# A gated linear attention with a mixture of experts: every engine's order written by hand for the last four attention units and the early expert block

## The chip, the cores and the metric

The kernel runs on one core of a Trainium2 chip. The metric is the device time of one execution in microseconds (us). A core has TensorE (PE) for matmuls, VectorE (DVE), ScalarE (ACT), GpSimd (POOL) and SyncE (SP), each working through its own instructions in their order, and DMA queues that they feed.

## The reference

First an attention-like recurrence for 4 batches, 8 heads, 768 steps and head size 40; then a mixture of 16 experts (4 groups of 4) over its 3072 rows of 320 numbers, where each row goes to the best expert of its best group.

```python
for t in range(S):
    m_new = np.maximum(f_gate[:, :, t] + m, i_gate[:, :, t])
    f_stab, i_stab = np.exp(f_gate[:, :, t] + m - m_new), np.exp(i_gate[:, :, t] - m_new)
    C = f_stab * C + i_stab * einsum('bhd,bhe->bhde', vt, kt)
    n = f_stab * n + i_stab * kt
    y[:, :, t] = sigmoid(o_gate[:, :, t]) * einsum(C, qt) / max(|n . qt|, 1.0)
x = y as 3072 rows of 320
g_idx = argmax(x @ w_group); e_idx = argmax(x[g] @ w_expert[g])   # per row
out[row] = softmax weights of g_idx and e_idx * (max(x[row] @ w1[g, e], 0) @ w2[g, e])
```

## The kernel before

**Attention.** The steps are cut into 6 chunks of 128 and each chunk into its 4 batches, which makes 24 units, numbered 0 to 23 (unit u is chunk u // 4 of batch u % 4). A unit has these steps: `loads` (SP), `decays` (a mask `upper` on POOL, eight exponentials on ACT), `scores` (PE, tile `sp`), `masked` (DVE, tile `pt`, two halves), `carried` and `carried2` (PE `it`, DVE `num`: the part of the state), `values` (PE, `av`), `norm` to `norm3` and `rows` (DVE: the unit's 128 finished rows, tile `x`), `turn` (ACT, SP: the store of `x` to the DRAM tensor `x_d`; PE: three transposes `tp`; ACT: `xT`), and `logits` (PE, `lg`: scores of the 4 groups and 16 experts for each row). A unit's last steps are done during the next unit or the one after.

**Routing.** `route` takes the logits of some units and finds each row's expert, weight and place in the expert's list, on DVE, with an exponential on ACT and some small matmuls on PE (ranks and counts); it is a generator, and the loop takes a piece of it now and then (`go_on`). `put_id` writes 128 rows' numbers and weights (`tokw`) into the lists in DRAM (`itab`), an indirect DMA by POOL. In chunk 4 (units 16 to 19) the route is in two parts, units 16 to 18 and unit 19; in chunk 5 likewise, units 20 to 22 and unit 23.

**The early block.** The two most loaded experts are picked after the third chunk, and their weights loaded and split early (`early_loads`, `early_splits` and `lows`: each fp32 matrix becomes a high part, cast on ACT, and a low part, subtracted on DVE, so that three fast products replace a slow one). The first picked expert does its first 256 rows as soon as the lists of units 0 to 19 are in DRAM: POOL loads its list (`load_ix`, tile `ix`), gathers the rows (`load_x`, tile `xg`, two gathers of 128), PE turns them (`tpm`), ACT and DVE split them (`xhl`), and `early_expert` does both layers (`psh`, then `hh` on ACT and DVE, then `po`). Its 128 late rows are gathered (list `li`) when the last lists are in DRAM, and follow as `expert((0, 1), ...)`. `all_experts` sorts the other 14 experts by load; each is done by `expert` with weights two experts ahead in flight.

**What sets the order.** Up to unit 21 the code's order is each engine's order (`manual_schedule`). Units 22 and 23 and the whole early block stand outside it: there a scheduler orders each engine by its own estimate, guided by `issue_after` and `high_priority`. From `expert((0, 1), ...)` on, the code's order holds again. Two things bear on DRAM order: `no_order` declares stores, gathers and scatters to distinct rows independent, and the second expert's `w2` is the tail of `early_loads`:

```python
    with tc.issue_after(rt["xs"].ins):
        do(early_loads)
```

where `rt["xs"]` is the store of the last unit's `x`. `busy(n)` issues n matmuls whose result nobody reads.

Of the kernel before, what the change touches and what calls it, by code (L numbers as in the profile page):

```python
# [40 lines left out]
CAPS = [EARLY + LATE, 352, 320, 288, 256, 256, 256, 256, 192, 192, 192, 192, 160, 160, 160, 128]  # L41

# [8 lines left out]
def lstm_moe(ctx: ExitStack, tc: tile.TileContext, gates, qkT, nat, og, wcat, w1, w2, cst, out):  # L51
# [55 lines left out]
    rt = {"manual": True}  # L107
# [58 lines left out]
    def decays(u):  # L166
        c, b = divmod(u, B)
        ab = st_[u]["ab"]
        upper(ab, NEG)
# [4 lines left out]
        for j in range(H):  # L174
            rt["exp"] = nc.scalar.activation(ab[:, j, :], ab[:, j, :], AF.Exp, bias=bcol[:, c, b * H + j:b * H + j + 1])  # L175

    def scores(u):
        t = st_[u]
        qk = t["qk"]
        t["pm"] = []  # L180
        for hh in range(2):
# [71 lines left out]
    def values(u):  # L253
        t = st_[u]
        nt = t["nt"]
        av = ps_1.tile([P, 512], F32, name="av")
        for j in range(H):
            o = j * D1
            mm(av[:, o:o + P], t["pm"][j // 4][:, j % 4, :], nt[:, o:o + P], start=True, stop=True)  # L259
        t["av"] = av  # L260
# [22 lines left out]
    def norm3(u):  # L283
# [4 lines left out]
        (nc.gpsimd if u < 20 else nc.vector).tensor_tensor(sr, sigs[c][:, b, :].rearrange("p (h d) -> p h d", d=D),  # L288
# [8 lines left out]
    def turn(u):  # L297
# [3 lines left out]
        rt["xs"] = ins = nc.sync.dma_start(x_d[b * S + c * P:b * S + (c + 1) * P, :], x)  # L301
        if c == NCH - 1:
            no_order("early", ins)
        tp = ps_1.tile([P, 3, P], F32, name="tp", tag="tp")
        for k in range(3):
            kk = min(P, DM - k * P)
            ins = nc.tensor.transpose(out=tp[0:kk, k, :], in_=x[:, k * P:k * P + kk], identity=ident)
        rt["tp", u] = ins
        if u > NU - 4:
            with tc.issue_after(ins.ins):  # L310
                busy(2)
# [8 lines left out]
    def logits(u):  # L320
# [3 lines left out]
        if u == NU - 1:  # L324
            rt["bank"] = ps_1.tile([P, B * 36 + NE], F32, name="lg2", tag="av")
        for k in range(3):
            kk = min(P, DM - k * P)
            rt["lg", u] = mm(rt["bank"][:, b * 20:(b + 1) * 20], st_[u]["xT"][0:kk, k, :], wc[0:kk, k, :],
                             start=(k == 0), stop=(k == 2))
# [7 lines left out]
    def route(c, b0, b1, bank):  # L337
# [11 lines left out]
        with ExitStack() as st:  # L349
            if not rt["manual"] and c == NCH - 2:  # L350
                st.enter_context(tc.issue_after(rt["exp"].ins))
# [507 lines left out]
    def unit(u):  # L859
# [14 lines left out]
        if u < MANUAL:  # L874
            go_on()
# [352 lines left out]
```

## Time and profile before

| | us |
|---|---|
| median of 3 runs | 444.68 (444.68 to 447.98) |
| the profiled execution | 447.25 |
| its span, first to last instruction | 445.7 |
| PE busy | 408.4 |
| DVE busy | 314.1 |
| ACT busy | 270.6 |
| POOL busy | 189.0 |

Times in the rows below are us from the start of the span. The profiled execution is 2.57 us longer than the median and 1.55 us longer than its own span. The attention part ends near 180 us, the early block runs to about 215 us, the other 14 experts take the rest. On the page's 40 slices the PE row stands at 9 nearly throughout; the slice that begins at 178 us stands at 4.

### The profile page before, as it was taken

The page shows a single profiled execution, that of the slowest core. Times are in us where ns is not written, and L with a number is a line of the kernel's source. Part 1 is how long each engine was busy: PE and PEld are TensorE (multiplying, and loading weights), DVE is VectorE, ACT ScalarE, POOL GpSimd, SP SyncE. Part 2 cuts the span into 40 slices and gives each one's busy share as a digit, 9 for nine tenths or more (in the row PEclk, how much of TensorE's full clock was granted, in tenths as well). Part 3 has the DMA queues.
Part 4 walks back from the last instruction along what each step waited for, and adds up shares of the span by engine and source line. Part 5 has one row for each costly group of instructions (what it writes and reads, how often), then busy time and mean ns, then how long its engine had stood idle before and what let it go on. Part 6 is the DMA issues. An engine that isn't in the chain of part 4 may idle for free.

```text
span 445.7 us, 9295 instructions
## 1 busy us (share of the span) xinstructions
PE 408.4 (92%) x3324; PEld 390.2 (88%) x3324; DVE 314.1 (70%) x731; ACT 270.6 (61%) x602; POOL 189.0 (42%) x215
## 2 busy tenths in 40 slices
PE   7599999997998999499999999999999999999970
PEld 4599999986997998299999999999999999999960
DVE  6755876658759798375474656756677999999950
ACT  5559556485476653134473655755676888888840
POOL 7454657474664472425523224234223333343120
PEclk9989999998999899689999999999999999999995
DMA  5998987989599941535385566386567676777000
GB/s 155 305 302 279 305 193 217 300 216 278 163 316 306 318 153 37 171 136 165 124 317 193 183 239 203 133 306 215 193 237 273 236 244 233 257 283 280 17 24 1
DMA packets 29908, 94.73 MB, mean 213 GB/s; under 512 B 9169, under 2 KB 13226, under 8 KB 26276
## 3 DMA queue, kind: packets, MB, share of 16 engines
q1 hardware_dynamic: 24804, 79.59, 55.5%
q0 software_dynamic: 4784, 14.18, 9.2%
q8 instruction: 27, 0.44, 0.4%
q10 hardware_dynamic: 272, 0.36, 0.3%
q14 instruction: 21, 0.17, 0.1%
HBM read 84.14 MB, written 10.82 MB: 213 GB/s over the span
## 4 chain that ended last, share of the span: by engine, by line
PE 63%; issue 11%; POOL 9%; DVE 7%; DMA 4%; ACT 1%; POOLq 0%; SPq 0%; DVEq 0%; ACTq 0%
PE psh L690 24%; PE po L733 6%; PE po L734 6%; PE po L735 6%; PE sp L185 4%; PE po L739 2%; PE psh L710 2%; PE po L738 2%; PE psh L631 2%; POOL sr L288 2%; PE it L211 2%; DMA xg<-x_d,ix 2%; POOL kw L198 2%; POOL itab L453 2%; DMA w1s<-in_w_dram 1%
## 5 line engine op out<-in xcount | busy, mean ns | idle before, releaser
L551 POOL DMA_INDIRECT out_dram<-y,ix x34 | 44.8, 1319 | 132.6 <-ACT y L747 121.3
L690 PE MATMUL psh<-xhl,w1h 128*128 128x256 f32 (+4 forms) x368 | 85.4, 309 | 0.0
L175 ACT ACTIVATE ab<-ab,bcol 128x128 f32<-128x128 f32 x184 | 56.3, 388 | 13.9 <-POOL ab L147 13.3
L733 PE MATMUL po<-w2h,hh 128*128 128x320 f32 (+1 forms) x192 | 60.7, 316 | 0.0
L690 PEld LDWEIGHTS psh<-xhl,w1h 128*128 128x128 f32 x368 | 59.9, 189 | 0.0
L734 PE MATMUL po<-w2l,hh 128*128 128x320 f32 (+1 forms) x192 | 59.3, 309 | 0.0
L735 PE MATMUL po<-w2h,hh 128*128 128x320 f32 (+1 forms) x192 | 59.2, 308 | 0.0
L664 DVE TENSOR_TENSOR w2l<-w2s,w2h 128x640 fp32r<-128x640 f32 x64 | 51.8, 823 | 6.4 <-ACT w2h L660 5.4
L185 PE MATMUL sp<-qk 128*128 128x128 f32 x384 | 50.9, 287 | 4.9 <-DMA qk<-in_qkT_dram 4.9
L259 PE MATMUL av<-nt,pt 128*128 128x128 f32 x384 | 51.7, 288 | 0.9 <-DVE pt L191 0.8
L185 PEld LDWEIGHTS sp<-qk 128*128 128x128 f32 x384 | 47.3, 200 | 5.7 <-issue 2.8
L690 PE MATMUL psh<-xhl,w1l 128*128 128x256 f32 (+6 forms) x256 | 49.0, 273 | 0.0
L259 PEld LDWEIGHTS av<-nt,pt 128*128 128x128 f32 x384 | 46.6, 197 | 2.4 <-DVE pt L191 1.4
L783 DVE SCALAR_TENSOR_TENSOR hh<-psh,hh 128x512 fp32r<-128x512 f32 (+3 forms) x36 | 21.5, 615 | 36.5 <-ACT hh L780 36.5
L690 PE MATMUL psh<-xhl,wsk 128*128 128x256 f32 (+4 forms) x184 | 46.8, 304 | 0.0
L147 POOL TENSOR_SCALAR_AFFINE_SELECT ab<-ab 128x1024 f32<-128x1024 f32 (+1 forms) x25 | 27.1, 1083 | 45.0 <-DMA ab<-a_d 38.3
L660 ACT CAST w2h<-w2s 128x640 fp32r<-128x640 f32 x64 | 45.0, 723 | 0.0
L547 POOL DMA_INDIRECT xg<-x_d,ix x34 | 36.1, 1061 | 18.6 <-DMA ix<-itab 7.1
L690 PEld LDWEIGHTS psh<-xhl,w1l 128*128 128x128 f32 x256 | 42.5, 189 | 0.0
L664 DVE TENSOR_TENSOR w1l<-w1s,w1h 128x1024 fp32r<-128x1024 f32 x32 | 38.9, 1219 | 3.7 <-ACT w1h L660 3.6
L191 DVE TENSOR_TENSOR pt<-sp,ab 128x512 f32<-128x512 f32 x48 | 32.9, 685 | 10.2 <-PE sp L185 8.2
L780 ACT ACTIVATE hh<-psh 128x512 fp32r<-128x512 f32 (+3 forms) x28 | 18.0, 644 | 31.0 <-PE psh L690 31.0
(183 smaller groups left out, 888.0 us busy)
## 6 DMA issues: line engine op xcount, KB each, us to landing
w1s<-in_w_dram SPq DMA_DIRECT2D x12, 1536.0 KB
w2s<-in_w_dram SPq DMA_DIRECT2D x13, 1280.0 KB
ab<-a_d SPq DMA_DIRECT2D x23, 512.0 KB
nt<-in_nat_dram SPq DMA_DIRECT2D x24, 324.0 KB
qk<-in_qkT_dram SPq DMA_DIRECT2D x48, 160.0 KB
x_d<-x SPq DMA_DIRECT2D x24, 192.0 KB
sig<-in_og_dram SPq DMA_DIRECT2D x6, 640.0 KB
w1s<-in_w_dram SPq DMA_DIRECT2D x4, 768.0 KB
```

The lines of the kernel that those rows point to most:

```text
L175: rt["exp"] = nc.scalar.activation(ab[:, j, :], ab[:, j, :], AF.Exp, bias=bcol[:, c, b * H + j:b * H + j + 1])
L185: mm(sp[:, jj, :], qk[:, j % 2, j // 2, :], qk[:, 2, j // 2, :], start=True, stop=True)
L191: nc.vector.tensor_tensor(pt, t["pm"][hh], t["ab"][:, 4 * hh:4 * hh + 4, :], op=ALU.mult)
L259: mm(av[:, o:o + P], t["pm"][j // 4][:, j % 4, :], nt[:, o:o + P], start=True, stop=True)
L547: return nc.gpsimd.indirect_dma_start(out=o, out_offset=None, in_=src, in_offset=bass.IndirectOffsetOnAxis(ap=idx, axis=0))
L551: return nc.gpsimd.indirect_dma_start(out=out, out_offset=bass.IndirectOffsetOnAxis(ap=idx, axis=0), in_=y, in_offset=None, bounds_check=N ...
L660: nc.scalar.copy(t[names[0]][:, dst], src[r][:, s])
L664: nc.vector.tensor_tensor(o, src[r][rows, s], h.bitcast(F32), op=ALU.subtract)
L690: mm(ps[:, g, 0:n_], w[:, s], x, start=(n == 0), stop=(n == len(todo) - 1))
L733: mm(po[0:m], hh[:, f, t], w2h[:, s], start=st0, stop=False)
L734: mm(po[0:m], hh[:, f, t], w2l[:, s], start=False, stop=False)
L735: mm(po[0:m], hh[:, f, tl], w2h[:, s], start=False, stop=sp0)
```

## The change

The scheduler's part is gone: units 20 to 23 are written out in `last_units`, and the early block's side work in the generator `lists`, of which `early_expert` takes a piece after every half and every whole pair of feature blocks. The last units are routed as 16 to 18, 19, 20 and 21, 22 and 23. Unit 19's `logits` stand in unit 20 and its route in units 20 and 21. The low parts of the first expert's w2 (three of four), until now in units 20 to 23, stand in the early block between the `hh` steps, and the selection of the experts behind them. The third expert's `w1` and `w2` are asked for after the gathers for the second. `turn` of the late rows stands before the last two of the eight feature blocks, formerly before the third. The store of `x` and the gathers are declared independent of each other but not among themselves.

```diff
-        (nc.gpsimd if u < 20 else nc.vector).tensor_tensor(sr, sigs[c][:, b, :].rearrange("p (h d) -> p h d", d=D),
+        (nc.gpsimd if u < HAND - 1 else nc.vector).tensor_tensor(sr, sigs[c][:, b, :].rearrange("p (h d) -> p h d", d=D),
...
-        ends = {B - 1: 0} if c < NCH - 2 else {B - 2: 0, B - 1: B - 1}
-        if b in ends:
-            chores.insert(0 if c < NCH - 2 else len(chores), route(c, ends[b], b + 1, rt["bank"]))
+        if b == B - 1 and c < NCH - 2:
+            chores.insert(0, route(c, 0, B, rt["bank"]))
...
                 for n, (w, s, x) in enumerate(todo):
                     mm(ps[:, g * W:(g + 1) * W], w[:, s], x, start=(n == 0), stop=(n == len(todo) - 1))
+                if g == 0:
+                    steps(lists, 1)
...
+            steps(lists, 1)
+        after()
...
-                if f == NF // 4 and i == len(blocks(W)) - 1:
-                    with tc.issue_after(ins.ins):
-                        do(last)
+                if f == NF - 2 and i == len(blocks(W)) - 1:
+                    do(last())
...
-        for _ in range(1 if u < 20 else 3):
+        for _ in range(4 if u == HAND - 1 else 1):
             put_id()
+
+    def last_units():
+        a, b, c, d = range(HAND, NU)
+        loads(d)
+        decays(c, "upper")
+        norm(a - 1)
+        scores(a)
+        norm1(a - 1)
+        masked(a, 0)
+        norm2(a - 1)
+        carried(a)
+        logits(a - 2)
+        r1 = route(NCH - 2, 0, B - 1, rt["bank"])
+        masked(a, 1)
+        norm3(a - 1)
+        rows(a - 1)
+        steps(r1, 1)
+        carried2(a)
+        steps(r1, 3)
+        values(a, (0,))
+        turn(a - 1)
+        values(a, (1,))
+        steps(r1, 1)
+        logits(a - 1)
+        r2 = route(NCH - 2, B - 1, B, rt["bank"])
+        decays(c, "exp")
+        steps(r1, 5)
+        put_ids()
+        steps(r1, 1)
+
+        norm(a)
+        scores(b)
+        steps(r2, 4)
+        norm1(a)
+        masked(b, 0)
+        steps(r2, 1)
+        carried(b)
+        steps(r2, 3)
+        masked(b, 1)
+        steps(r2, 2)
+        put_ids()
+        decays(d, "upper")
+        load_ix(0, nc.gpsimd)
+        xgs[0] = load_x(EARLY, ix_of(0), True)
...
+        carried(d)
+        logits(b)
+        r3 = route(NCH - 1, 0, 2, rt["bank"])
+        masked(d, 1)
+        steps(r3, 4)
+        carried2(d)
+        norm3(c)
+        rows(c)
+        values(d, (0,))
+        steps(r3, 1)
+        values(d, (1,))
+        turn(c)
+        xl = early_turn((0, 0), EARLY, xgs[0], ((ps_a, "it"), (ps_s, "sp")))
+        norm(d)
+        norm1(d)
+        norm2(d)
+        norm3(d)
+        rows(d)
+        do(xl)
+        logits(c)
+        steps(r3, 5)
+        put_ids()
+        busy(2)
+        turn(d)
+        do(early_loads)
+        steps(r3, 1)
+        busy(2)
+        logits(d)
+        rt["r4"] = route(NCH - 1, 2, B, rt["bank"])
+        steps(rt["r4"], 4)
...
+        def lists():
+            steps(rt["r4"], 6)
+            put_ids()
+            lreg = nc.values_load(late_i[0:1, 0:1], engines=[ET.SP], min_val=0, max_val=NSLOT - P,
...
+            xgs[0, 1] = load_x(LATE, rt["late"])
+            xgs[1] = load_x(CAPS[1], ix_of(1))
+            yield
+            for _ in range(2):
+                yield
+                do(lows, 1)
+                yield
+            yield
+            do(lows)
+            experts = all_experts()
+            next(experts)
+            load_e(2, [ET.SP, ET.Pool])
+            load_ix(2)
+            load_w1(2, nc.gpsimd)
+            load_w2(2, nc.gpsimd)
+            yield
+            next(experts, None)
+            yield
```

How this moves instructions, at three places.

POOL, at the entries of unit 19 into the lists (`itab`), before:

```order
L453 DMA itab<-tokw,slot 49280x2
L452 MEMSET sep 1x1 x5
L453 DMA itab<-tokw,slot 49280x2
L580 ISA
L580 DMA ix<-itab 128x3x2
L547 DMA xg<-x_d,ix 128x384 x2
L453 DMA itab<-tokw,slot 49280x2 x4
L557 TENSOR_LOAD ewi
L565 ISA
L565 DMA w1s<-in_w_dram 128x3072
```

and after:

```order
L447 DMA itab<-tokw,slot 49280x2
L446 MEMSET sep 1x1
L447 DMA itab<-tokw,slot 49280x2
L150 AFFINE_SELECT ab<-ab 128x1024
L579 ISA
L579 DMA ix<-itab 128x3x2
L546 DMA xg<-x_d,ix 128x384 x2
L446 MEMSET sep 1x1
L447 DMA itab<-tokw,slot 49280x2
```

Unit 19's entry, the list's load and the gathers keep their sequence; the mask of unit 23 (AFFINE_SELECT) now stands between the entry and the list's load, which before stood ahead of all of these.

PE, where the gathered rows are turned (`tpm`), before:

```order
L374 LDWEIGHTS ones_b
L374 MATMUL lg<-ohsum_77,ones_b 128x48
L328 MATMUL lg_2554<-wc,xT 128x20
L611 MATMUL tpm<-cs,xg 128x128 x6
L114 LDWEIGHTS ones_b
L114 MATMUL busy<-ones_b 128x512
```

and after:

```order
L267 MATMUL av<-nt,pt 128x128 x4
L314 MATMUL tp<-cs,x 128x128 x2
L314 MATMUL tp<-cs,x 64x128
L610 MATMUL tpm<-cs,xg 128x128 x6
L329 MATMUL lg<-wc,xT 128x20 x3
L117 LDWEIGHTS ones_b
L117 MATMUL busy<-ones_b 128x512
```

The transposes of the gathered rows stood behind every unit's `logits` (`lg_2554` is unit 23's) and directly ahead of the first expert product; now they stand behind unit 22's `tp`, with the logits of units 22 and 23 and unit 23's `tp` behind them.

DVE, from a step `hh` of the early expert to the late rows' low part `xhl`, before:

```order
L634 SCALAR_TENSOR_TENSOR hh<-psh,hh 128x2x256
L535 TENSOR_TENSOR ovr<-cntr,off 128x16
L536 TENSOR_SCALAR ovr<-ovr 128x16
L538 CAST ovi<-ovr 128x16
L539 TENSOR_SCALAR ovi<-ovi 128x16
L540 CAST ovr<-ovi 128x16
L542 TENSOR_REDUCE tot_f<-ovr 128x1
L543 CAST total<-tot_f 128x1
L634 SCALAR_TENSOR_TENSOR hh<-psh,hh 128x2x256 x2
L664 TENSOR_TENSOR w1l<-w1s,w1h 128x1024 x2
L664 TENSOR_TENSOR wsk<-w1s,wsk 64x1024
L614 TENSOR_TENSOR xhl<-tpm,xhl 128x3x128
```

and after:

```order
L528 TENSOR_TENSOR big<-sel,cntf 128x256
L529 TENSOR_REDUCE cntr<-big 128x16
L534 TENSOR_TENSOR ovr<-cntr,off 128x16
L535 TENSOR_SCALAR ovr<-ovr 128x16
L537 CAST ovi<-ovr 128x16
L538 TENSOR_SCALAR ovi<-ovi 128x16
L539 CAST ovr<-ovi 128x16
L541 TENSOR_REDUCE tot_f<-ovr 128x1
L542 CAST total<-tot_f 128x1
L667 TENSOR_TENSOR w1l<-w1s,w1h 128x1024 x2
L667 TENSOR_TENSOR wsk<-w1s,wsk 64x1024
L613 TENSOR_TENSOR xhl<-tpm,xhl 128x3x128
```

Before, two `hh` steps stood between the last selection step (`total`) and the low parts of the second expert's w1; now the fourth `hh` stands ahead of the whole second half of the selection, and that directly ahead of `w1l`.

## Rows read from the trace of the kernel before

**Rows 1.** Windows of the span. Columns: stretch (us from the span's start); its length and PE's busy time with the count of instructions; then PEld, DVE, ACT and POOL in the same way; the granted clock of TensorE (1.00 is its upper level of 2.4 GHz, 0.50 its lower of 1.2 GHz); the DMA share; GB/s.

```profile
180.00:185.00 5.00, 1.19 (x5) 0.69 (x5) 1.59 (x10) 0.48 (x1) 3.16 (x4) 0.66 0.90 321
...
185.00:190.00 5.00, 3.07 (x11) 1.77 (x12) 1.42 (x10) 0.60 (x2) 0.00 (x0) 0.50 0.03 8
...
215.00:236.00 21.00, 21.00 (x142) 20.75 (x141) 12.86 (x16) 11.94 (x19) 9.50 (x10) 1.00 0.69 234
```

**Rows 2.** The timeline of PE from the last units to the first expert product. Columns here and in every timeline below: start, length (us), engine, line, operation, output<-input, shapes, count, and in brackets how long the engine stood idle before and what ended it.

```profile
176.21 0.95 PE L328 MATMUL lg<-wc,xT 128*128 128x20 f32 x6
...
177.96 0.52 PE L307 MATMUL tp<-cs,x 128*128 128x128 f32 x3 [0.80 <-DVE df L347]
...
179.90 0.40 PE L328 MATMUL lg<-wc,xT 64*128 64x20 f32 x2
...
182.86 0.90 PE L611 MATMUL tpm<-cs,xg 128*128 128x128 f32 x3 [2.57 <-DMA xg<-x_d,ix]
...
186.76 0.90 PE L611 MATMUL tpm<-cs,xg 128*128 128x128 f32 x3 [3.00 <-DMA xg<-x_d,ix]
...
189.11 0.98 PE L631 MATMUL psh<-xhl,w1h 128*128 128x256 f32 x3 [0.17 <-DVE oh L361]
```

**Rows 3.** The timeline of POOL: the last list entry of unit 19, the list's load, the first gather, the last list entry of all, the late gather.

```profile
170.61 1.29 POOL L453 DMA_INDIRECT itab<-tokw,slot  x1 [2.37 <-DVE tokw L405]
...
174.85 0.81 POOL L580 DMA_DIRECT2D ix<-itab  x1 [2.95 <-DMA itab<-tokw,slot]
...
177.97 1.00 POOL L547 DMA_INDIRECT xg<-x_d,ix  x1 [2.32 <-DMA ix<-itab]
...
191.48 0.96 POOL L453 DMA_INDIRECT itab<-tokw,slot  x1 [6.69 <-DVE slot L403]
...
197.12 1.00 POOL L547 DMA_INDIRECT xg<-x_d,li  x1 [1.40 <-DMA li<-itab]
```

**Rows 4.** The gather's line L547 in the stretch from 170 to 215 us, its last line: from issue to landing.

```profile
DMA to landing us min/median/max: 3.6/4.6/7.4
```

**Rows 5.** The timeline of SP's queue: five stores of x, then the two halves of the second expert's w2.

```profile
158.42 20.02 SPq L301 DMA_DIRECT2D x_d<-x  x5
...
178.64 0.88 SPq L565 DMA_DIRECT2D w2s<-in_w_dram  x2
```

**Rows 6.** The timeline of ACT: the eight exponentials of unit 23's decays, then the route of unit 19; and the first relu of the early expert.

```profile
165.76 2.44 ACT L175 ACTIVATE ab<-ab,bcol 128x128 f32<-128x128 f32 x8
...
168.11 0.20 ACT L352 ACTIVATE ex<-df 128x20 f32<-128x20 f32 x1
...
192.68 0.60 ACT L633 ACTIVATE hh<-psh 128x512 fp32r<-128x512 f32 x1 [4.38 <-PE psh L631]
```

**Rows 7.** The timeline of DVE: the last step of the route of units 16 to 18, and that of unit 19.

```profile
163.22 0.15 DVE L405 TENSOR_TENSOR tokw<-sm,se 128x3 f32<-128x3 f32 x1
...
170.18 0.15 DVE L405 TENSOR_TENSOR tokw<-sm,se 128x1 f32<-128x1 f32 x1
```

**Rows 8.** One window: from unit 20's scores to the end of unit 22's logits (columns as in rows 1).

```profile
151.00:177.16 26.16, 25.63 (x218) 24.13 (x216) 22.54 (x86) 14.15 (x38) 12.30 (x22) 1.00 0.45 143
```

**Rows 9.** The timeline of DVE: first and last step of the four that turn logits into one-hot rows, of units 20 to 22.

```profile
177.20 0.22 DVE L345 TENSOR_REDUCE mx<-lg 128x15 f32<-128x60 f32 x1
...
178.76 0.21 DVE L365 TENSOR_TENSOR oh<-oh 128x48 bf16<-128x48 f32 x1
```

**Rows 10.** One window: the first expert's first layer, 64 matmuls and a few small ones (columns as in rows 1).

```profile
189.11:198.11 9.00, 9.00 (x70) 8.91 (x70) 7.22 (x36) 1.80 (x3) 2.52 (x3) 0.85 0.19 54
```

**Rows 11.** The timeline of PE: the first matmul of the early expert's second layer, the transposes of the late rows, the first matmul of the late block.

```profile
198.11 0.31 PE L645 MATMUL po<-w2h,hh 128*128 128x320 f32 x1
...
202.57 0.55 PE L611 MATMUL tpm<-cs,xg 128*128 128x128 f32 x3
...
205.60 0.28 PE L690 MATMUL psh<-xhl,w1h 128*128 128x256 f32 x1
```

**Rows 12.** The timeline of DVE: one quarter of a w2 low part; then, in the early block, the first and the last step of the expert selection with one hh and the six equal small steps' first among them, the low parts of the second expert's w1, and the late rows' low part.

```profile
163.38 0.82 DVE L664 TENSOR_TENSOR w2l<-w2s,w2h 128x640 fp32r<-128x640 f32 x1
...
190.51 0.17 DVE L459 SCALAR_TENSOR_TENSOR key<-cntf,keyb 128x16 f32<-128x16 f32 x1
...
193.31 0.69 DVE L634 SCALAR_TENSOR_TENSOR hh<-psh,hh 128x512 fp32r<-128x512 f32 x1 [0.65 <-ACT hh L633]
...
195.84 0.17 DVE L535 TENSOR_TENSOR ovr<-cntr,off 128x16 f32<-128x16 f32 x1
...
197.08 0.15 DVE L543 CAST total<-tot_f 128x1 int32<-128x1 f32 x1
...
199.87 2.36 DVE L664 TENSOR_TENSOR w1l<-w1s,w1h 128x1024 fp32r<-128x1024 f32 x2 [0.24 <-ACT w1h L660]
...
202.26 1.22 DVE L664 TENSOR_TENSOR wsk<-w1s,wsk 64x1024 fp32r<-64x1024 f32 x1
...
203.68 0.56 DVE L614 TENSOR_TENSOR xhl<-tpm,xhl 128x384 fp32r<-128x384 f32 x1 [0.19 <-ACT xhl L613]
```

**Rows 13.** The timeline of PE: the end of the longest other wait of the attention part.

```profile
105.97 0.19 PE L370 MATMUL lg<-oh,lt_b 128*128 128x64 bf16 x1 [3.01 <-DVE oh L365]
```

**Rows 14.** Two windows of 1 us after it (columns as in rows 1).

```profile
106.00:107.00 1.00, 1.00 (x15) 1.00 (x15) 0.85 (x5) 1.00 (x5) 0.00 (x0) 0.74 1.04 421
...
109.00:110.00 1.00, 1.00 (x7) 1.00 (x7) 0.72 (x4) 0.00 (x0) 0.00 (x0) 0.55 0.98 266
```

More of the change, by code (lines that the diff above doesn't have):

```diff
@@ L613, in one, with early_expert @@
             nc.scalar.copy(xh, tp[:, :, 0:m])
-            nc.vector.tensor_tensor(xhl[:, :, 1, i * P:i * P + m], tp[:, :, 0:m], xh.bitcast(F32), op=ALU.subtract)
-        return [lambda i=i, m=m: one(i, m) for i, m in enumerate(blocks(W))]
-    def early_expert(W, ws, idx, after, last):
+            t["low"].append(lambda: nc.vector.tensor_tensor(xhl[:, :, 1, i * P:i * P + m], tp[:, :, 0:m],
+                                                            xh.bitcast(F32), op=ALU.subtract))
+        for i, m in enumerate(blocks(W)):
+            one(i, m)
+        return t["low"]
+    def early_expert(W, ws, idx, lists, after, last):
         w1h, w1l, wsk, w2h, w2l = (ws[n] for n in ("w1h", "w1l", "wsk", "w2h", "w2l"))
@@ L918, in unit, with steps @@
             gate_o(u // B + 1)
-        for _ in range(1 if u < 20 else 3):
+        for _ in range(4 if u == HAND - 1 else 1):
             put_id()
+    def steps(g, n):
+        for _ in range(n):
+            next(g, None)
+    def last_units():
[40 more added lines that the diff above has]
+        xgs[0] = load_x(EARLY, ix_of(0), True)
+        norm2(a)
+        carried2(b)
+        norm3(a)
+        rows(a)
+        steps(r2, 1)
+        values(b)
+        do(early_splits, 2)
+        norm(b)
+        scores(c, (0,))
+        turn(a)
+        scores(c, (1,))
+        decays(d, "exp")
+        norm1(b)
+        masked(c, 0)
+        norm2(b)
+        carried(c)
+        logits(a)
+        masked(c, 1)
+        carried2(c)
+        norm3(b)
+        rows(b)
+        values(c, (0,))
+        turn(b)
+        values(c, (1,))
+        do(early_splits)
+        steps(early_counts(), 9)
+        norm(c)
+        scores(d)
+        norm1(c)
+        masked(d, 0)
+        norm2(c)
+        carried(d)
[28 more added lines that the diff above has]
+        steps(rt["r4"], 4)
@@ L1022, in lstm_moe @@
     with tc.manual_schedule():
-        for u in range(2, MANUAL):
+        for u in range(2, HAND):
             unit(u)
@@ L1070, in lstm_moe @@
-    load_ix(1)
-    load_e(2, [ET.SP, ET.Pool])
-    load_ix(2)
-    next(experts, None)
-    for r in range(NEARLY):
-        xgs[r, 1] = load_x(LATE, late_ix[r])
-    xgs[1] = load_x(CAPS[1], ix_of(1))
-    load_w1(2, nc.gpsimd)
-    load_w2(2, nc.gpsimd)
-    own, rest = casts(1)
-    def second_w1():
-        for act, low in own:
-            act()
-            low()
-    early_expert(EARLY, wsp_[0], ix_of(0), second_w1, turn_tasks((0, 1), LATE, xgs[0, 1]))
-    pools["ps_o_"].close()
-    first_banks.close()
@@ new lines, in second_w1 @@
+        def second_w1():
+            for act, low in own:
+                act()
+                low()
+        early_expert(EARLY, wsp_[0], ix_of(0), lists(), second_w1, lambda: early_turn((0, 1), LATE, xgs[0, 1], [(ps_1, "tp")]))
+        early_banks.close()
+        first_banks.close()
+        pools["ps_h"] = enter(tc.tile_pool(name="ps_h2", bufs=3, space=PSUM, reuse_waits="tile"))
+        pools["ps_o"] = enter(tc.tile_pool(name="ps_o2", bufs=2, space=PSUM, reuse_waits="tile"))
+        pools["late"] = True
@@ L1094, in lstm_moe @@
+        expert((0, 1), LATE, rt["late"], [], (), lambda: turn2(1, CAPS[1], xgs[1]))
         own = rest
```

164 lines of the change are left out of this document (61 added, 103 removed).

## The prediction

> **What bounds the kernel now.** I read the page's slices first: PE is busy almost throughout, with one hole at 178 to 189 us. The windows show the hole and what surrounds it: PE works 1.19 of the 5 us from 180 and 3.07 of the next 5, at a granted clock of 0.66 and 0.50, while in the experts' stage it is busy 21.00 of 21 us at full clock [rows 1]. So a microsecond won before about 205 us reaches the end whole, if it is won on PE. The hole's causes are on PE's timeline: the last unit's logits end at 180.3, the gathered rows arrive in two pieces at 182.86 and 186.76 (idle 2.57 and 3.00, both ended by the gather's DMA), and the first expert product starts at 189.11 [rows 2]. The chain behind it lies on POOL: unit 19's entry into the lists at 170.61, released by DVE's `tokw`; the list's load 4.24 later; the first gather 3.12 after that [rows 3]. A gather of this stretch lands 3.6 us after its issue at best, 4.6 in the median, 7.4 at worst [rows 4]. The worst one is the second gather of the hole; the second expert's w2 goes out at 178.64, in the middle of it [rows 5].
>
> **The change part by part.**
>
> *Unit 19 routed at once.* Before, its exponential stood on ACT behind the eight of unit 23's decays and began at 168.11 [rows 6], so `tokw` came at 170.18, while the route of units 16 to 18 was ready at 163.22 [rows 7]. Now its logits precede unit 21's scores and its DVE steps follow those of units 16 to 18, with one unit's `pt`, `num` and `x` between. I put its `tokw` at about 163.5, an estimate: the time at which the first part ended before, since the first part no longer shares DVE with two w2 low parts. Entry 163.8; the mask of unit 23, now between entry and list load, ends while the entry lands; list load 168.0, gathers 171.2 and 172.5, the second landed between 176 and 177 (180 with the worst latency). The w2 transfer still goes out behind the last store of x, as it did before [rows 5]: this third of the change moves no instruction past another on SP, and is worth only the separation that the earlier gather gives.
>
> *PE up to the first product.* From unit 20's scores to unit 22's logits PE was busy 25.63 of 26.16 us [rows 8], so the new order can't gain there; it can lose. It works through the same matmuls; two turned blocks come in and four idle fillers go out, which I call even. New waits that the written order makes, walked through engine by engine: unit 19's small rank matmuls wait for their one-hot rows behind unit 21's scores (about 0.9); the half-unit interleaving of `turn` and `values` waits for x (0.2 to 0.3, three times); the ranks of units 20 and 21 stand between the halves of unit 23's `values` and wait for one-hot rows that can't begin before unit 21's logits (0.5). From logits to one-hot rows is 1.77 us on DVE [rows 9], some 1.3 of it without the other unit's work between. The sum is 2.0 to 2.4 more than the 0.5 idle before: unit 22's logits end at 179.2 instead of 177.1. Before, the last unit's logits ended 3.1 later [rows 2]; with 2.3 here, since the fillers and the transposes of unit 23 lie in what was waiting, the first product starts at **181.5, not 189.11: 7.6 earlier**. The gather's 177 is just in time for its place ahead of unit 22's logits (178).
>
> *First layer.* It took 9.00 us at a mean clock of 0.85 [rows 10], so 7.65 at full clock. New in it: the ranks of units 22 and 23 stand after the first eight matmuls (under 1 us) and wait for their one-hot rows, which start only when the last logits are out and DVE has finished the route of 20 and 21: 1.0 of waiting. 8.65, to 190.1 instead of 198.11.
>
> *Second layer and the late block.* From there to the late block's first product was 7.49 us, all of it PE work [rows 11]; PE would be ready at 197.6. But the late rows' low part `xhl` must be there, and DVE's queue now reaches it later. Before, the three w2 low parts (0.74 us from one start to the next [rows 12]) lay in the attention part, and the selection between the `hh` steps while PE multiplied. Now DVE does hh, w2l, hh, w2l, hh, w2l, the selection's first half, the fourth hh, its second half, w1l twice, wsk, xhl. The third hh starts at 189.0 (third product pair at 188.25, ACT's relu 0.6 [rows 6]): 0.6 for it, 0.75 for w2l. The selection from `key` to `total` took 6.7 from 190.51 to 197.23 with two `hh` of 0.6 in it, 0.65 idle and two small strangers, so 4.65 alone; one hh on top makes 5.25 [rows 12]. That is 195.6. Then w1l and wsk, 3.6 from 199.87 to the end of wsk, and xhl 0.56 [rows 12]: 199.7. The steps that depend on each other lose the fillers that stood between them, 0.3 to 0.6: **200.2**. PE idles 2.5 us at the late block, which starts 5.4 earlier than 205.60. The late gather itself is not the bound: the last entry of a list goes out near 187, and 5.64 later [rows 3] the gather, landed by 197.
>
> *The clock.* A hole of this size has a price of its own. The longest other one, 3.01 us before 105.97 [rows 13], was followed by a granted clock of 0.50 from about 106.5 to 109.5 [rows 14], that is 1.2 instead of 2.4 GHz for 3.0 us of work-bound time: 1.5 us lost. The holes of 2.57 and 3.00 in question did the same [rows 1, 2]. Holes of 0.5 in all, in the last attention units, cost nothing: the clock there is 1.00 [rows 8]. 2.5 is nearer to the former, so I charge the 1.5.
>
> Sum: 5.4 - 1.5 = 3.9. The profiled execution becomes 447.25 - 3.9 = 443.35; it lay 2.57 above the median, and the forecast against the median is 444.68 - 3.9 = **440.8**. Everything after the late block is taken as unmoved: each weight load is released by a cast that PE's progress paces, and the third expert's w1, now asked for behind the gathers, has some 15 us until its first cast.
>
> A figure that would change this: the Trainium skill, Perfetto Trace Analysis, section "Optimizing Scalar/DVE Operations", states about 60 ns of access overhead for a DVE instruction on SBUF and a profiled latency of about twice that. The six equal steps from 195.84 to 197.08 stand 0.21 apart [rows 12], hence the trace doesn't agree for steps that depend on each other. By the page's 0.12, an estimate, some twenty such steps would be 1.8 shorter, the hole 0.7, the clock would hold, and the sum would be 7.2: 437.5.
>
> **The rivals.**
>
> *The clock holds through the hole.* A fall needs more than a gap: The 0.80 us before 177.96 [rows 2] passed without one until the next hole came. If 2.5 after 16 us of dense work passes too, the gain is 5.4: 439.3.
>
> *DVE is not late.* Were the selection to run in 3.0 us instead of 5.25, by steps that overlap, xhl would be ready when PE is and the gain would be nearly the whole 8.0 by which PE is ready earlier (205.60 less 197.6), 437. For it speaks only that DVE idled 0.65 among these steps before, so that some of their spacing is not their own. The Trainium skill's figure above, in Perfetto Trace Analysis, is this case.
>
> *The hand order waits more than walked.* Each unit has five handovers between PE, ACT and DVE, and the old scheduler overlapped two units freely; at 0.1 more for each of twenty handovers the first product comes 2 us later, and PE, thinned out around 180, falls to the lower clock once more for 1.5. Gain 3.9 - 3.5 = 0.4: 444.3.
>
> *Slower: the gather is no earlier.* `tpm` now stands ahead of the logits of units 22 and 23 and of unit 23's transposes, which before were done by 180.3. If the gathered rows land as late as before, at 186.7, these are behind them: about 4.5 at the lower clock to the first product, 191.2, so 2.1 late instead of 7.6 early, with the 1.0 and 2.5 of the two new waits on top: 450.3. The mechanism would be a list load that waits on POOL for a transfer that is not among those on POOL's timeline [rows 3]. It decides from a landing at about 183 on; my walk has 177.
>
> *It doesn't do what it says* holds for w2 alone, as said, and costs nothing.
>
> **How the numbers follow.** Forecast with the clock falling 0.42 (440.8; by the bounds of the waits 439.8 to 442.2); clock holding 0.27 (439.3); DVE not late 0.08 (437); more waits 0.17 (444.3); slower 0.06 (450). A measurement of this kernel tells about 1% from no change, 4.4 us: faster than 440.2 are the second and third case and a seventh of the first, 0.41; over 449.1 lies only the last, 0.05 of it; the rest 0.54. The range leaves out the slower case and the outer halves of the two next: 437.5 to 444.3.
>
> **What would show it.** Right: unit 19's list entry near 164 on POOL and both gathers landed before 178; PE's first expert product at 181 to 182 without a wait of over 1 us on a gather; a wait of PE for DVE's `xhl` of 2 to 3 us at the first late product, near 200; granted clock at 0.50 for some 3 us after it. Wrong: gathers still the last thing before the first product; a late block that starts straight behind the second layer (then the gain is larger); or several holes between 157 and 181 (then smaller).

## The result, and the profile after

The changed kernel takes 449.11 us in the median of 19 runs (445.01 to 454.39), the kernel before 444.72 beside it. The ratio is 1.008, with a 95% interval of 1.0052 to 1.0109: slower by 0.5 to 1.1%, where 440.8, 0.9% faster, was forecast. Runs that the chip disturbed are left out of the ratios, and where the profiled run of a kernel below is such a one (the second bank, the pause with three moves), only stretches of it are read. The profiled execution took 451.05 us, its span is 449.5 (445.7 before).

PE's timeline around the new first product, with its waits in brackets; it answers to [rows 2]:

```profile
151.82 1.95 PE L191 MATMUL sp<-qk 128*128 128x128 f32 x16
...
157.76 0.87 PE L314 MATMUL tp<-cs,x 128*128 128x128 f32 x3 [1.33 <-DVE mx L345]
...
164.31 0.17 PE L367 MATMUL lg<-oh,lt_b 128*128 128x16 bf16 x1 [0.69 <-DVE oh L362]
...
170.35 0.55 PE L314 MATMUL tp<-cs,x 128*128 128x128 f32 x3 [1.80 <-DVE x L301]
...
182.67 0.82 PE L610 MATMUL tpm<-cs,xg 128*128 128x128 f32 x6
...
186.47 0.92 PE L329 MATMUL lg<-wc,xT 128*128 128x20 f32 x6 [0.88 <-DVE pr L395]
187.32 0.74 PE L633 MATMUL psh<-xhl,w1h 128*128 128x256 f32 x4
```

The gathered rows are no bound any more: `tpm` starts without a wait. Yet the first product comes at 187.32, 1.8 us earlier than before (189.11), not 7.6. From unit 20's scores at 151.82 it is 35.50 us (38.1 before). The two longest waits stand ahead of the turns of units 19 and 20. (The first is put down to `mx`, the step that starts behind `x` on DVE; `x` of unit 19 ended at 157.61, 0.15 ahead of the turn.) DVE and POOL show why. First DVE, then POOL, around the finished rows of unit 20 (and `sr` of unit 19 and of unit 21 for comparison; `sr` is the output gate divided by `den`, the last thing that `x` needs):

```profile
155.26 1.82 DVE L295 TENSOR_TENSOR sr<-sig,den 128x320 f32<-128x320 f32 x1
...
167.69 2.08 DVE L295 TENSOR_TENSOR sr<-sig,den 128x320 f32<-128x320 f32 x1
169.80 0.49 DVE L301 TENSOR_TENSOR x<-num,sr 128x320 f32<-128x320 f32 x1
...
173.32 0.49 DVE L295 TENSOR_TENSOR sr<-sig,den 128x320 f32<-128x320 f32 x1
```

```profile
155.63 1.10 POOL L150 TENSOR_SCALAR_AFFINE_SELECT ab<-ab 128x1024 f32<-128x1024 f32 x1
...
167.34 0.95 POOL L447 DMA_INDIRECT itab<-tokw,slot  x1 [1.09 <-DVE den L288]
168.30 1.11 POOL L150 TENSOR_SCALAR_AFFINE_SELECT ab<-ab 128x1024 f32<-128x1024 f32 x1
...
172.31 0.81 POOL L579 DMA_DIRECT2D ix<-itab  x1 [2.89 <-DMA itab<-tokw,slot]
...
176.17 1.00 POOL L546 DMA_INDIRECT xg<-x_d,ix  x1 [3.05 <-DMA ix<-itab]
177.47 0.95 POOL L546 DMA_INDIRECT xg<-x_d,ix  x1 [0.30 <-issue]
```

The same product of the same size takes 0.49 us for unit 21, but 1.82 and 2.08 for units 19 and 20, and both long ones end 0.35 us after a mask on POOL ends. PE's turn needs `x`. Unit 19's `sr` is on DVE by the change itself: before, POOL did it, in 0.72 at 155.82.

At the early block's end, the last work of DVE and the late block's first product (they answer to [rows 12] and [rows 11]), then the clock (columns as in [rows 1]):

```profile
202.33 0.15 DVE L542 CAST total<-tot_f 128x1 int32<-128x1 f32 x1
202.44 2.36 DVE L667 TENSOR_TENSOR w1l<-w1s,w1h 128x1024 fp32r<-128x1024 f32 x2
204.83 1.22 DVE L667 TENSOR_TENSOR wsk<-w1s,wsk 64x1024 fp32r<-64x1024 f32 x1
206.08 0.56 DVE L613 TENSOR_TENSOR xhl<-tpm,xhl 128x384 fp32r<-128x384 f32 x1
```

```profile
206.70 0.58 PE L693 MATMUL psh<-xhl,w1h 128*128 128x256 f32 x1 [2.63 <-DVE xhl L613]
...
213.99 1.07 PE L713 MATMUL psh<-cs,xg 128*128 128x128 f32 x9
```

```profile
155.00:160.00 5.00, 3.67 (x22) 3.45 (x22) 4.69 (x15) 3.13 (x9) 1.74 (x3) 0.77 0.94 280
160.00:165.00 5.00, 4.31 (x39) 4.01 (x39) 3.33 (x18) 3.06 (x9) 2.11 (x4) 0.89 0.26 67
...
205.00:210.00 5.00, 3.30 (x15) 3.31 (x16) 1.97 (x3) 0.37 (x1) 2.71 (x4) 0.55 0.92 320
210.00:215.00 5.00, 5.00 (x37) 5.00 (x36) 1.98 (x7) 2.06 (x6) 0.00 (x0) 0.77 0.90 350
```

The late block starts 1.1 us later than before (206.70 for 205.60) and its first layer takes 7.29 instead of 4.65 us at the fallen clock. 1.1 + 2.64 is 3.74 of the 3.8 by which the span grew. So all that the change gained ahead of the hole was given back in DVE's queue, and in this execution the hole then cost the clock as well.

### The profile page after: what moved, and what is told of

It reads as the page before. It is cut to its first block, busy times and chain, and to the rows that moved or that the text cites. A ratio compares the mean times of both kernels' runs of the same rounds, so it can differ in the third digit from the quotient of the medians.

```text
span 449.5 us, 9283 instructions
## 1 busy us (share of the span) xinstructions
PE 409.5 (91%) x3319; PEld 392.0 (87%) x3319; DVE 321.9 (72%) x730; ACT 270.7 (60%) x602; POOL 187.3 (42%) x214
## 4 chain that ended last, share of the span: by engine, by line
PE 65%; DVE 12%; DMA 8%; issue 5%; POOL 5%; SPq 1%; ACT 1%; POOLq 0%; DVEq 0%; ACTq 0%
PE psh L693 24%; PE po L736 6%; PE po L737 6%; PE po L738 6%; PE sp L191 5%; PE av L267 3%; DMA nt<-in_nat_dram 2%; PE po L742 2%; PE psh L713 2%; PE it L217 2%; PE lg L329 2%; PE po L741 2%; DMA qk<-in_qkT_dram 2%; DMA itab<-tokw,slot 2%; DMA a_d<-A__117 2%
## 5 line engine op out<-in xcount | busy, mean ns | idle before, releaser
L693 PE MATMUL psh<-xhl,w1h 128*128 128x256 f32 (+4 forms) x368 | 87.5, 314 | 2.6 <-DVE xhl L613 2.6
L693 PEld LDWEIGHTS psh<-xhl,w1h 128*128 128x128 f32 x368 | 61.4, 193 | 2.9 <-DVE xhl L613 2.9
L267 PE MATMUL av<-nt,pt 128*128 128x128 f32 x384 | 52.6, 289 | 0.8 <-DVE pt L197 0.7
L693 PE MATMUL psh<-xhl,w1l 128*128 128x256 f32 (+6 forms) x256 | 49.9, 277 | 0.0
L693 PEld LDWEIGHTS psh<-xhl,w1l 128*128 128x128 f32 x256 | 43.8, 194 | 0.0
```

What stands on the lines that cost most here:

```text
L267: mm(t["av"][:, o:o + P], t["pm"][hh][:, jj, :], nt[:, o:o + P], start=True, stop=True)
L693: mm(ps[:, g, 0:n_], w[:, s], x, start=(n == 0), stop=(n == len(todo) - 1))
```

## The experiments

The theory: two things put the time where it is. A mask on GpSimd holds up a VectorE product beside it, which makes units 19 and 20 late, and VectorE's queue makes the late block late and drops the clock. Rivals: the waits are the price of the written order as such, or they are hidden by the gather or by the next wait. Times are read in two ways. The first is the median and its ratio to the kernel before, measured beside it; that kernel's own median was 444.72 beside the changed kernel and 445.13, 446.02 and 446.92 beside the experiments, so two kernels of different groups are compared by their ratios. The changed kernel's is 1.008, and a difference of less than about 0.5% between two ratios is not told from nothing. The second, since single runs of one kernel lie 5 us apart, is the distance from unit 20's scores to the first product in the profile (35.50 in the changed kernel).

**Masks earlier.** Both masks before the entries of units 16 to 18.

```diff
         loads(d)
-        decays(c, "upper")
...
-        decays(c, "exp")
+        decays(d, "upper")
+        decays(c, "upper")
         steps(r1, 5)
         put_ids()
...
         steps(r2, 4)
+        decays(c, "exp")
...
         put_ids()
-        decays(d, "upper")
         load_ix(0, nc.gpsimd)
```

> Edit: POOL's masks of units 22 and 23 are issued ahead of the list entries of units 16 to 18, in a stretch where POOL waits, instead of next to the DVE steps sr of units 19 and 20; unit 22's exponentials move behind unit 19's. Theory (POOL's mask and list entry hold DVE up: sr took 1.82 and 2.08 us beside them, 0.49 elsewhere): sr of unit 19 about 0.5 to 0.9, sr of unit 20 at most 1.1 (only the list entry is still beside it); PE's waits of 1.33 and 1.80 us for x of these units fall under 0.8 each, the clock does not fall near 158, the first expert product comes 2 to 3.5 us earlier, at 184 to 185.5, and the time falls by as much. Rival (sr is slow for what it reads or because of its place in DVE's queue): both sr stay at 1.8 to 2.1, the time stays.

455.02 us, ratio to the kernel before 1.0224 (1.0123 to 1.0325). `sr` fell to 0.49 and 0.75 and the waits for `x` to 0.33 and 1.07, so the hold-up is the masks' (the 0.75 stands beside one of them still). But POOL now waited for unit 23's decays, with the list entries queued behind:

```profile
163.60 2.13 POOL L150 TENSOR_SCALAR_AFFINE_SELECT ab<-ab 128x1024 f32<-128x1024 f32 x2 [8.35 <-DMA ab<-a_d]
...
177.33 0.80 POOL L579 DMA_DIRECT2D ix<-itab  x1 [6.38 <-DMA x_d<-x]
```

```profile
183.15 0.52 PE L610 MATMUL tpm<-cs,xg 128*128 128x128 f32 x3 [3.05 <-DMA xg<-x_d,ix]
```

The list load starts 5 us later than in the changed kernel, and the rows arrive after PE wants them. The last list entry went out 2.4 later (169.75 for 167.34); the row puts the end of the wait down to a store of `x`, and which of the two landings it was is not settled. This is the prediction's slower rival (the gather no earlier, with the logits queued behind `tpm`), brought about by the experiment: its price was real, its place was elsewhere.

**A bank of their own for the last logits.**

```diff
+        if u == NU - 2:
+            rt["bank"] = ps_1.tile([P, B * 36 + NE], F32, name="lg2", tag="av")
```

> Edit: the logits of units 22 and 23 go to a PSUM bank of their own, as unit 23's did in the kernel before. Theory (the last logits wait for DVE's product pr of the route of units 20 and 21 because both use one bank): the wait of 0.88 us at 186.47 goes, and the first expert product comes 0.7 to 0.9 earlier; time down by 0.5 to 1. Rival (they wait for ACT's copy xT of unit 23): the wait stays, the time stays.

448.73 us, 1.0084 (1.0037 to 1.013). The wait of 0.88 is gone; the wait of the ranks behind it grew from 0.37 to 0.68. From the turn of unit 20 to those ranks it is 18.09 instead of 18.55 us, so some 0.5 is won, which the ratio does not tell from nothing. Its profile shows two more things. Both `sr` are held as in the changed kernel (1.83 and 2.08), yet the clock stays at 1.00 from 155 to 220. The distance is 33.21, of which the wait of 0.88 explains 0.88: with that wait it would be 34.1. So some 1.4 of the changed kernel's 35.50 is the clock's fall behind unit 19, which did not come here although both masks are where they were. And behind the hole at the late block, 2.56 here, the clock did not fall either, and the first layer took 4.74:

```profile
210.05 0.39 PE L695 MATMUL psh<-xhl,w1h 128*128 128x256 f32 x1 [2.56 <-DVE xhl L615]
```

```profile
210.00:215.00 5.00, 4.95 (x42) 4.95 (x43) 1.93 (x5) 1.76 (x6) 1.37 (x2) 1.00 0.97 399
```

**Second half of the selection behind `xhl`.**

```diff
                     do(last())
+                    next(rt["experts"], None)
...
             yield
-            next(experts, None)
+            rt["experts"] = experts
             yield
```

> Edit: the second half of the expert selection stands behind the late rows' low part xhl on DVE, not ahead of the second expert's w1 low parts. Theory (the hole of 2.63 us ahead of the late block is DVE's queue, and the clock's fall after it costs as much again): xhl comes 3 to 3.9 earlier, the hole shrinks to what the late gather leaves (0.5 to 1), the clock stays at 1.00 through 205 to 215, the late block takes 4.7 us instead of 7.3, and the time falls by 4 to 5. Rival (the hole ends with the late gather or with ACT): hole 2 us or more, time within 1 us of the changed kernel's.

445.06 us, 1.0036 (1.0001 to 1.0071), by fourteen small steps on DVE moved behind four others: 4.05 below the changed kernel by the medians, 2.0 by the ratios, whose intervals just overlap. The hole is 0.28 instead of 2.63 (the late gather is waited for 0.74 instead of 0.51), and the clock holds:

```profile
202.85 0.39 PE L694 MATMUL psh<-xhl,w1h 128*128 128x256 f32 x1 [0.28 <-DVE xhl L613]
```

```profile
205.00:210.00 5.00, 4.71 (x40) 4.50 (x39) 4.10 (x16) 2.85 (x9) 1.14 (x2) 1.00 0.98 392
210.00:215.00 5.00, 5.00 (x35) 5.00 (x34) 1.47 (x4) 1.20 (x3) 1.10 (x2) 1.00 0.61 210
```

The late block's first layer takes 5.30 instead of 7.29, and not the 4.7 expected, since PE now waits for DVE within it (0.6 in all).

**Twelve idle matmuls in the hole.** They stand behind the last product of the second layer, and nobody reads them.

```diff
+        fl = ps_1.tile([P, 512], F32, name="fill", tag="lg")
+        for _ in range(12):
+            mm(fl, ones_b, bc(ones_b.unsqueeze(1), (P, 4, P)), start=True, stop=True)
```

> Edit: twelve fillers of 0.215 us (matmuls whose result nobody reads) stand in PE's order between the second layer and the late block, in the hole; nothing else moves. Theory (the hole itself costs 2.6, the clock's fall behind it another 2.6): the late block starts when xhl is there, as before, but runs in 4.7 us instead of 7.3 and the clock stays at 1.00; time down by 2 to 2.7. Rival (the clock falls anyway for the thin work before, or the late block is slow because of its own waits): the late block still takes over 6 us, time as the changed kernel's or 0.3 worse.

446.17 us, 1.0047 (1.0008 to 1.0086): 2.9 below the changed kernel by the medians, 1.5 by the ratios, with `xhl` as late as there. The clock of the two windows above is 1.00 and the late block's first layer takes 4.69. In the changed kernel's profile the clock's share of the hole's price, 2.64, is as much as the wait. That the idle matmuls keep the clock up is supported by the time as well, but one profile doesn't prove it, since with the second bank it stayed up without them.

**Mask of unit 23 behind the list load,** and its exponentials behind the turn of unit 21.

```diff
         put_ids()
-        decays(d, "upper")
         load_ix(0, nc.gpsimd)
+        decays(d, "upper")
...
-        decays(d, "exp")
...
         turn(b)
+        decays(d, "exp")
```

> The changed kernel with one thing moved: GpSimd masks unit 23's decays between the list load and the gathers (in the changed kernel it does so right behind the last list entry, at 168.30), and ScalarE's eight exponentials of that unit come behind the turn of unit 21 instead of before it. Theory A (a GpSimd mask beside a VectorE product of two SBUF operands holds the product up until the mask is over): unit 20's sr takes 0.5 to 1.0 us instead of 2.08, PE's wait for x of unit 20 falls from 1.80 to 0.3 to 0.8, the gathers start no later than 176.2 and 177.5, and the time falls by 1.0 to 1.5 us against the changed kernel (to about 447.7). Theory B (it is the list entry's own issue, at 167.34, that holds the product up, not the mask): sr keeps 1.2 us or more and the time is within 0.5 us of the changed kernel's. Theory C (later exponentials make the values of unit 23 late instead): sr is short, PE waits as long ahead of unit 23's values, and the time does not fall.

446.85 us, 1.0053 (1.0014 to 1.0093). `sr` of unit 20 takes 0.49 although the list entry lies beside it as before, so the entry does not hold `sr` up (theory B falls), and PE's wait for that `x` is 0.21. DVE, then POOL:

```profile
165.97 0.49 DVE L295 TENSOR_TENSOR sr<-sig,den 128x320 f32<-128x320 f32 x1
```

```profile
165.62 0.95 POOL L447 DMA_INDIRECT itab<-tokw,slot  x1 [1.09 <-DVE den L288]
```

Theory C was partly right: PE waits 0.46 more for unit 23's `pt` and 1.22 ahead of the ranks of units 20 and 21. From the scores to the first product: 33.99, 1.5 less than in the changed kernel, but no less than the 34.1 without the clock's fall. So what the move won at unit 20 (1.6) the later waits took back.

**One list entry fewer in unit 19,** so that unit 22's mask comes 1.3 us earlier.

```diff
-        for _ in range(4 if u == HAND - 1 else 1):
+        for _ in range(3 if u == HAND - 1 else 1):
```

> The changed kernel with one number: unit 19 issues three list entries instead of four, so that the fourth goes with those of units 16 to 18 and GpSimd's mask of unit 22 starts 1.3 us earlier (154.4 instead of 155.63), before unit 19's sr. Theory A (the mask holds up sr): sr of unit 19 takes 0.5 to 0.8 us instead of 1.82, PE's wait of 1.33 ahead of the turn of unit 19 shrinks to 0 to 0.4, the clock does not fall in the 10 us behind it, and the time falls by 1.0 to 1.6 us (to about 447.6). Theory B (what is lost there is given back later, since unit 19's list entry and unit 20's sr come in the same order as before and the entry of unit 19 is up to 0.2 later): the wait goes and the time moves by less than 0.5 us.

446.64 us, 1.0077 (1.0032 to 1.0122). `sr` of unit 19 takes 0.81 and the clock from 155 to 165 is 1.00 instead of 0.77 and 0.89; the distance is 33.99 again. But PE still waits 1.08 there, where 0 to 0.4 was expected. The 1.0 that `sr` won is on VectorE alone: in this profile its queue lay 0.8 further behind PE (`num` 2.10 after the start of unit 20's scores, 1.32 in the changed kernel). With the second bank PE waited 1.07 and the clock stayed up too, with `sr` at 1.83. So neither the distance (34.1 without the clock's fall) nor the time (1.0077 for 1.008) shows a gain; theory B fits.

**Four moves together:** mask of unit 23 behind the list load, three entries in unit 19, the second bank, the late half of the selection (the diffs above).

> The changed kernel with four moves together: mask of unit 23 behind the list load (and its exponentials behind the turn of unit 21), three entries in unit 19, the logits of units 22 and 23 in a PSUM bank of their own, and the second half of the expert selection behind the late block's low halves on VectorE. Theory A (each of the waits stands on the path, and the terms add): against the kernel with the selection alone moved (445.06) another 1.2 for unit 20, 1.2 for unit 19 and 0.4 for the bank, 442 to 442.6 us, 2 to 3 us faster than the kernel before. Theory B (the list chain becomes the bound once PE is early: list entry at 167.4, gathers at 176.2 and 177.5, landed at 179.5 and 181.2, while PE reaches the turn of their rows at about 180): a wait of 1 to 1.5 us ahead of the turn of the gathered rows takes the place of those removed, the clock may fall once, and the time is 443.5 to 445.5.

443.65 us, 0.998 (0.9939 to 1.0022): as fast as the kernel before, which measured 446.02 in that group, and 1.0% below the changed kernel by the ratios. The distance is 32.22, the late block's hole 0.28, and `tpm` of the early rows has no wait, so the list chain did not become the bound. The 1.04 ahead of the ranks, which the moved mask brings, is still there, and so is 0.97 at unit 19: the earlier mask of unit 22 now held `den` for 1.15, two steps ahead of `sr`.

**A pause on GpSimd.** Three clears of an unused tile between unit 19's entry and unit 23's mask; nothing is moved.

```diff
         put_ids()
+        idle = post.tile([P, 192], F32, name="idle", bufs=1)
+        for _ in range(3):
+            nc.gpsimd.memset(idle, 0.0)
         decays(d, "upper")
```

> The changed kernel with three clears of an unused 128x192 tile on GpSimd (about 0.7 us together, by 0.42 us for the 128x384 clear of its profile) between unit 19's list entry and unit 23's mask; nothing else moves, and the exponentials keep their place. In the changed kernel that mask starts 0.61 us after unit 20's sr. Theory A (what holds sr up is the mask that follows the entry, and clears that only write do not): sr of unit 20 takes 0.5 to 0.8 us, PE's wait for x of unit 20 falls from 1.80 to 0.2 to 0.6, the mask holds up a small step of den instead, which nothing waits for, and the time falls by 1.2 to 1.6 us against the changed kernel (to about 447.6), with no wait of 1.22 ahead of the ranks of units 20 and 21, as the later mask had. Theory B (the clears hold VectorE up as the mask does): sr takes 1.5 us or more and the time does not fall.

447.33 us, 1.0047 (1.0005 to 1.0089); distance 33.75. POOL, then DVE:

```profile
164.94 0.91 POOL L961 MEMSET idle<- 128x192 f32 x3
165.81 1.09 POOL L150 TENSOR_SCALAR_AFFINE_SELECT ab<-ab 128x1024 f32<-128x1024 f32 x1
```

```profile
164.33 0.49 DVE L295 TENSOR_TENSOR sr<-sig,den 128x320 f32<-128x320 f32 x1
164.86 0.49 DVE L301 TENSOR_TENSOR x<-num,sr 128x320 f32<-128x320 f32 x1
...
166.07 0.85 DVE L284 SCALAR_TENSOR_TENSOR den<-num 128x8 f32<-128x8 f32 x1
```

A microsecond of nothing lets `sr` and `x` pass; the mask now holds up a step on 8 numbers (0.85 for 0.17). It is not free: it lies on the way to unit 21's `x`, whose turn now waits 0.40. PE's wait for unit 20's `x` is 0.21 instead of 1.80, and the ranks behind wait 0.36. The ratio, 0.3% below the changed kernel's, does not tell the gain from nothing by itself; the rows show the cause.

**The pause with the three other moves.**

> The clears of the run above, three entries in unit 19, the logits' second bank and the late half of the selection together: the kernel of four moves with the pause in place of the moved mask. Against that kernel (443.65) the wait of 1.04 ahead of the ranks of units 20 and 21 should go, so theory A gives 442.6 to 443.2, 0.5% or more below the kernel before. If the clears hold VectorE up, it is 444.5 or more.

439.02 us (six of its seven runs 436.27 to 441.04), 0.9843 (0.979 to 0.9895): some 10 below the changed kernel and faster than the one before by 1.0 to 2.1%. The distance is 31.88, and the ranks of units 20 and 21 wait 0.36 instead of 1.04. The wait at unit 19 is 0.97, with `den` held for 1.15 as before. The time is lower than the 442.6 to 443.2 expected; where the rest comes from stays open.

**Both halves of unit 20's values ahead of unit 19's turn,** on top of that.

```diff
-        values(a, (0,))
+        values(a)
         turn(a - 1)
-        values(a, (1,))
```

> The kernel above with both halves of unit 20's values ahead of unit 19's turn on PE (in the changed kernel one half stands on either side). There PE waits 0.97 to 1.33 us for x of unit 19 with the other half's 0.95 us of products ready behind it. Theory A: the wait goes and 0.5 to 0.9 us with it. Theory B: the next thing on PE, the ranks of units 16 to 18 or those of unit 19, waits on VectorE for as long (they already wait 0.16 and 0.69), and the time does not move by 0.3 us.

441.37 us, 0.9903 (0.9864 to 0.9941). The wait ahead of the turn shrinks from 0.97 to 0.64 and the ranks behind it wait 1.05 instead of 0.16: theory B, VectorE is what both wait for. It isn't a clean test: in its profile the decays of unit 22 landed late, and beside the mask `x` of unit 19 took 1.26 us.

## Why the prediction was wrong, point by point

- **Unit 19 routed at once: right in kind, late in size.** `tokw` came at 166.92 instead of 163.5 and the gathers at 176.17 and 177.47 instead of 171.2 and 172.5 ([rows 3]: 177.97 for the first before). It sufficed: PE wanted the rows only at 182.67. The walk forgot what the same order does to DVE: its queue stood idle for 1.36 us until PE had unit 19's logits at 161.6, which wait for unit 19's `x`, and all the route's later steps stand behind that.
- **PE up to the first product: the step that failed.** Forecast 181.5, measured 187.32. Of the 5.8, 0.8 is that unit 20's scores began later (the kernels above, with nearly the same code ahead of it, have them anywhere between 148.05 and 157.17). The stretch from there to the end of unit 22's logits took 32.48 instead of 28.2, and the rest to the first product 3.0 instead of 2.3. Of the 4.3 in that stretch, 2.0 are waits (PE was idle 4.6, by the walk 2.6), 1.4 the clock (PE was busy 27.89, and 26.46 for the same 225 matmuls at a clock of 1.00 with the second bank), and 0.8 what the walk had called even (26.46 for 25.63 in [rows 8]). The term "waits for x (0.2 to 0.3, three times)" measured 1.33, 1.80 and 0.34, and with the masks away from `sr` 0.33 (masks earlier) and 0.21 (mask of unit 23 later) for the first two; the ranks of unit 19 waited 0.69 (0.9 forecast), those of units 20 and 21 0.36 (0.5). In the walk each DVE step had its usual duration, and the mask on POOL cost nothing. Not priced were the hold-up of `sr`, the clock's fall to 0.77 from 155 to 160 and 0.89 to 165, and the 0.88 us by which the last logits waited for DVE's reading of `pr` in the bank they write to.
- **The missed rows.** The trace before had the sign, and I did not read it. A step of `den` on 8 numbers, mostly 0.16 us (seven of its 24 rows take 0.35 to 0.99), beside a mask (DVE, then POOL, in the kernel before):

```profile
137.48 0.99 DVE L281 TENSOR_SCALAR den<-den 128x8 f32<-128x8 f32 x1
```

```profile
137.35 1.09 POOL L147 TENSOR_SCALAR_AFFINE_SELECT ab<-ab 128x1024 f32<-128x1024 f32 x1 [2.22 <-DMA ab<-a_d]
```

  and in the same trace unit 20's `sr` and the mask of POOL miss each other by 0.1 us:

```profile
160.40 0.49 DVE L288 TENSOR_TENSOR sr<-sig,den 128x320 f32<-128x320 f32 x1
```

```profile
160.99 1.09 POOL L147 TENSOR_SCALAR_AFFINE_SELECT ab<-ab 128x1024 f32<-128x1024 f32 x1 [0.51 <-DMA ab<-a_d]
```

  For unit 20 the change left these operations as they were and moved one onto the other; unit 19's `sr` it took from POOL and put on DVE, beside unit 22's mask. I cost the mask between entry and list load at nothing because the entry was landing meanwhile: the cover was looked for on POOL's own chain, not on DVE. The Trainium skill, SBUF — State Buffer, section "SBUF: two separate sides", has the rule that I should have weighed: VectorE and GpSimd share one pair of ports under an exclusive lock for a whole instruction, and a VectorE operation with two SBUF inputs contends with a GpSimd operation that reads SBUF. The rows agree on the hold: 0.49 becomes 1.82 and 2.08. By the same section of the Trainium skill the operation that starts first gets the pair; by their recorded starts `sr` was first, by 0.37 and 0.61, and was held all the same.
- **First layer: right.** 8.65 forecast, 8.4 measured (187.32 to the second layer's first product at 195.73), though the wait in it was 0.37 and not 1.0.
- **The hole at the late block: right in size, and right in cause.** 2.5 forecast, 2.63 measured, and the selection's removal from ahead of `xhl` took it away. It came 6.5 later than forecast, nearly all of it the lateness of the first product; 0.51 was a wait for the late gather, which I had as no bound. That the size held is in part luck: PE and `xhl` both came some 0.6 later behind the first product than walked.
- **The clock: right here, too small, and not certain.** 1.5 forecast from [rows 13, 14], 2.64 measured, and 2.9 given back by the idle matmuls (1.5 by the ratios). The two kernels with one mask moved, with holes of 2.53 and 2.55, had a first layer of 6.29 and 6.30, 1.6 more than 4.65; with the second bank a hole of 2.56 cost 0.1. So the price of one such hole was between nothing and 2.6, and no single figure would have been right.
- **The rivals.** "The hand order waits more than walked" was the nearest, at 444.3 with a chance of 0.17, and still too cheap; its mechanism, 0.1 more at each of twenty handovers, is not what came, which is two long waits. "DVE is not late" fell: dependent small steps stand 0.21 apart in the new order too (201.92, 202.12, 202.33). "The clock holds" fell in this profile, and came true with the second bank. The slower rival had the wrong mechanism here: the gather came in time.
- **The sum.** 3.9 of gain was forecast: 5.4 earlier at the late block, less 1.5. Measured: 1.1 later and 2.64 of clock, 3.7 of loss. The difference of 7.6 is 6.5 at the late block, 5.8 of it at the first product, and 1.1 of clock.

## What to carry to other kernels

When a change moves instructions in time, look on every engine for operations that slow one another when they stand side by side, and read their longest durations, not their usual ones: a median hides the one row that tells. In a queue that takes on moved work, look for the one step that another engine waits for and put it first: that alone was worth 2 to 4 us here. A hole that ends in front of dense PE work can cost the clock on top of the wait, here anything from nothing to as much again, so it belongs in the forecast as a range. And before a gain is put down to an edit, see how much the same stretch differs in the profile of a kernel that left it alone: here the clock alone made 1.4 us.

## What the runs showed of the hardware

The mask (128x1024, 1.1 us) on GpSimd holds some VectorE operations until it has ended. `sr` on 320 numbers takes 0.75 to 2.08 instead of 0.49 and `x` 1.26 instead of 0.49, and they end 0.34 to 0.36 us after the mask's recorded end; `den` on 8 numbers takes 0.43 to 1.15 instead of 0.16 or 0.17 and ends 0.02 to 0.05 after it. Not every operation is held: `pt`, which reads PSUM, keeps 0.68, and the reciprocal 0.19 to 0.20, beside a mask. A list entry (0.95) or three clears (0.91) beside `sr` or `x` leave them at 0.49. But a list entry is not without effect on every step: in the changed kernel a small step `sm` beside one takes 0.35 (188.98) instead of 0.17 and ends 0.02 before the entry does. The recorded start of a mask is not to be relied on: `sr` of unit 20 began 0.61 us before it, would have ended 0.12 before it, and was held all the same.

The clock did not answer to the wait's length alone. PE's wait ahead of unit 19's turn was 1.33 in the changed kernel with the clock falling to 0.77 behind it, and 2.09 in the kernel with the pause with 1.00 behind it. At the late block holes of 2.53, 2.55 and 2.63 were followed by 0.67, 0.66 and 0.50 in the 5 us behind them, and one of 2.56 by 1.00. What else differs between them is not settled.
